# One FFT stream beside the first unit only, and Strassen's scheme for the second unit too

## The chip, the core and the metric

The kernel runs on one core of a Trainium2 chip. Times are device microseconds of one execution. TensorE (PE) does the matrix products, VectorE (DVE) and ScalarE (ACT) the element-wise work and the copies out of PSUM, GpSimd (POOL) some subtractions and additions between SBUF tiles. DMAs are issued on SP's queue (loads, outputs) and on ACT's (stores of results that are read again).

## The reference

Eight sequences of 3008 tokens and 256 channels go through a Fourier layer, and then through a mixer of tokens and channels.

```python
X = np.fft.rfft(x, axis=1)
Yr = X.real @ w_r - X.imag @ w_i + b_r
Yi = X.real @ w_i + X.imag @ w_r + b_i
Yr, Yi = (np.sign(Y) * np.maximum(np.abs(Y) - 0.01, 0) for Y in (Yr, Yi))
x = np.fft.irfft(Yr + 1j * Yi, n=3008, axis=1)          # (8, 3008, 256)

h = np.maximum(x.transpose(0, 2, 1) @ w_tok1, 0) @ w_tok2     # 3008 -> 256 -> 3008
u = x + h.transpose(0, 2, 1)
out = u + np.maximum(u @ w_ch1, 0) @ w_ch2                    # 256 -> 1536 -> 256
```

## The kernel before

**Precision.** A product is made from three matmuls in a 32-bit format of reduced precision: an operand is split into a high part (copied, by ACT as a rule) and the rest (a subtraction, by DVE or POOL), and `mm3` (lines 196 to 198) issues high x high, high x rest and rest x high.

**Units.** The eight sequences are five units: `[0]`, `[1]`, `[2, 3]`, `[4, 5]`, `[6, 7]`. A unit passes through a *spectral stream* (all that is done up to the token mixer's first product) and then through *channel mixing*.

**The spectral stream** of a unit is a generator, `spectral(u)`, that yields after each piece of PE work an estimate of its time. It first makes a DFT of length 47 in 13 groups (`dft47`: load `x`, sum and difference `sd`, split into `xh` and `xl`, PE product `p`, copy `a`, store to `a_d`). Units 3 and 4 have their DFT done within the steps of the unit before (`beside`). Then come 12 steps `kp`, with one or two sequences each: load `a`, PE `px` (`forward`), ACT copies `xf`, POOL adds a third part to `xf`, ACT and DVE split it into `xth` and `xtl`, PE `pm` (`mix`, the weights in the frequency domain), DVE `z` (bias and threshold), ACT and POOL split that into `y` and its rest (`yh`, `yl` with two sequences), PE `pi` (`inverse`) with the copy `bt` and its store to `b_d`, and PE `gp` (`tokens`). In unit 1 each step also splits the matrices `wt` (ACT, POOL) and `et` (ACT, DVE) and stores them for the later units. The stream ends with `g` in DRAM.

**Channel mixing** goes through a list of chunks of tokens. A token mix `make_u` (PE `pu`, line 860) makes the next chunk's `u` ahead of time from `wt2`, `g` and `b2`. There are two forms:

- `channel(n)`, chunks of up to 512 tokens: for each of 12 blocks of 128 features 6 matmuls of the first layer (`ph`), ACT and DVE make `hh` and `hlo` (lines 898, 899), and 6 matmuls of the second layer (`po`) two blocks later.
- `channel7(ns)`, chunks of up to 1024 tokens: Strassen's scheme for the first layer. For each pair of feature blocks, 7 products of 3 matmuls over half the tokens (`sx`, `sw`, `sq`, `sz`), with sums on DVE and copies on ACT between them (`sn`), in place of 8. The second layer is as before. `weigh` and `sum_u` make the summed operands.

Unit 0 is in 7 chunks of 470 or 376 tokens, since with it the float64 matrix `w_tok2` is read in pieces (`raw`), narrowed, split, and kept for the others. Unit 1 is in a chunk of 448 and five of 512. Units 2 to 4 are in wide chunks.

**Memory.** `raw`, `x` and `a` come from one ring of three buffers (`ld`). Before the first wide chunk the stream's pools are closed and their memory is taken by those of the Strassen stage (`open_seven`), so by then the stream has to be done. What is left of it at that point runs alone (`run(sp)`).

**What sets the order.** The loop at the end of the kernel draws on both generators. After each piece of mixing (an estimate `c`, counted down in `left_c`) it runs pieces of the stream while `left_s > pace * left_c`. `pace` is the ratio of what is left of the two, set anew after a `"wait"` (a unit's start), which holds the stream for 10 us of mixing. For unit 0 the stream's share is 2.1 times the estimate for a one-sequence unit; the rest lies beside unit 1.

Of the kernel before, what the change touches and what calls it, by code (L numbers as in the profile page):

```python
# [32 lines left out]
CW = 512  # L33
# [6 lines left out]
SPECTRAL = 70.3 + NG * (SLOW - 0.7)  # L40
# [86 lines left out]
def tile_kernel(ctx: ExitStack, tc: tile.TileContext, io):  # L127
# [650 lines left out]
    chunks = []  # L778
    for u, bs in enumerate(UNITS):
        total, at = N * len(bs), 0  # L780
        if u == 0:
            widths = [k * TOKS for k in sizes]
        elif u == 1:
            widths = [total % CW] + [CW] * (total // CW)
        else:
            plain = 0 if u == 2 else 0
            rest = total - plain
            widths = [plain % CW] * (plain > 0) + [CW] * (plain // CW) + [rest % CW7] + [CW7] * (rest // CW7)
        for cw in widths:
            chunks.append((u, at, cw))  # L790
            at += cw
        assert at == total
# [296 lines left out]
    def channel7(ns):  # L1089
        channels.close()  # L1090
        wc["tail"] = ctx.enter_context(tc.tile_pool(name="tail", bufs=1, reuse_waits="tile"))
        behind = None
        half = NF // 2
        for n in ns:
            after = n + 1 if n + 1 < len(chunks) else None
            mine = list(needs[after]) if after else []
            for p in range(half):
                hs = first7(n, p)
                if behind:
                    second7(*behind, 0, (0, 1))  # L1100
                if p < len(mine):
                    make_u(mine[p])
                    if p + 1 < len(mine):
                        load_wt2(mine[p + 1])
                        load_b2(mine[p + 1])
                if p == half - 2:
                    load_ahead(n + 2)
                if behind:
                    second7(*behind, 1, (0, 1))
                    if p == 0:  # L1110
                        for k in range(2):
                            finish7(behind[0], k, 2)
                behind = n, p, hs
                if after and p == half - 2:
                    sum_u(after)
                    for i in range(2):
                        split_u7(after, i)
                if after and p == half - 1:
                    for i in range(2, 7):
                        split_u7(after, i)  # L1120
        for k in range(2):
            for f in range(2):
                second7(*behind, f, (k,))
            finish7(behind[0], k, 2 - k)

    def run(gen):
        for _ in gen:
            pass
# [5 lines left out]
    spent, left_s, left_c, pace, hold = done, 0.0, 0.0, 0.0, None  # L1134
    first_wide = min(n for n, (_, _, cw) in enumerate(chunks) if cw > CW)

    def mixing(lo, hi):
        slots = sum(groups[g][3] for n in range(lo, hi) for g in needs[n + 1])
        return sum(32.7 * cw / CW for _, _, cw in chunks[lo:hi]) + 3.6 * slots * TOKS / GW

    for n, (u, at, cw) in enumerate(chunks):
        if n == first_wide:
            channel7(range(n, len(chunks)))
            break
        if at == 0 and u < 2:
            if u == 0:
                left_s = 2.1 * SPECTRAL - spent
                left_c = mixing(0, sum(cu == 0 for cu, _, _ in chunks))
            else:
                left_s = 3 * SPECTRAL + 4 * 70.3 - spent  # L1150
                left_c = mixing(n, first_wide - 1)
            pace, hold = 0.0, left_c - (25.0 if u == 0 else 0.0)
        for c in channel(n):
            if c == "end":
                if chunks[n + 1][2] > CW:
                    run(sp)
                    left_s = -1e9
                else:
                    while gts[u + 1] is None:
                        step = next(sp)  # L1160
                        if step != "wait":
                            left_s, spent = left_s - step, spent + step
                continue
            left_c -= c
            if hold is not None:
                if left_c > hold:
                    continue
                pace, hold = left_s / max(left_c, 1.0), None
            while left_s > pace * left_c:
                step = next(sp, None)  # L1170
                if step is None:
                    left_s = -1e9
                elif step == "wait":
                    hold = left_c - 10.0
                    break
                else:
                    left_s, spent = left_s - step, spent + step
# [36 lines left out]
```

## Time and profile before

| | |
|---|---|
| runs shown | 2396.96, 2398.89, 2388.59 us; median 2396.96 |
| the profiled execution | 2399.55 us, its span 2397.8 us |
| PE busy | 2360.6 us, 98% |
| DVE, ACT, POOL busy | 1417.6, 1143.3, 252.7 us |
| DMA | 277 MB, 116 GB/s in the mean |

The times agree within half a per cent, which is what one can hope to resolve. A matmul's row overlaps the next one, so a busy PE may still be one that is delayed a little at each step, and its cost is best read from the distance of the rows. The spectral stream can be told in any table by POOL, which does nothing else after the start.

### The profile page before, as it was taken

How to read it: one execution, taken by the hardware profiler on the slowest of the kernel's cores; microseconds unless marked ns; L12 is line 12 of the kernel's file. 1: busy time of each engine (PE TensorE's matmuls, PEld its weight loads, DVE VectorE, ACT ScalarE, POOL GpSimd, SP SyncE). 2: the span in 40 equal slices, each digit the busy share in tenths (PEclk: the TensorE clock that was granted, in tenths of full speed). 3: DMA queues.
4: the chain of work that ended last, by engine and by line, in shares of the span. 5: the costliest groups of instructions: out<-in, count | busy, mean ns of one | idle time of the engine just before them, and what ended most of it. 6: DMA issues, size and time to landing. Idle time of an engine off the chain costs nothing.

```text
span 2397.8 us, 32249 instructions
## 1 busy us (share of the span) xinstructions
PE 2360.6 (98%) x12524; PEld 2063.7 (86%) x12524; DVE 1417.6 (59%) x2220; ACT 1143.3 (48%) x2033; POOL 252.7 (11%) x223
## 2 busy tenths in 40 slices
PE   8999999999999999999999999999999999999999
PEld 7778899999988888898988888898888889888887
DVE  7966766655646564555555555555555555555554
ACT  6754445544434443433444444444444444444543
POOL 0000332232323322330000000000000000000000
PEclk9999999999999999999999999999999999999999
DMA  8765467655555545433213112122311112222100
GB/s 217 237 222 158 152 205 241 198 167 181 176 181 169 185 149 171 141 128 126 64 60 91 57 49 61 37 81 60 91 57 38 52 57 82 60 86 60 40 1 36
DMA packets 149766, 277.06 MB, mean 116 GB/s; under 512 B 10933, under 2 KB 94477, under 8 KB 149613
## 3 DMA queue, kind: packets, MB, share of 16 engines
q1 hardware_dynamic: 115225, 208.40, 29.5%
q10 hardware_dynamic: 34388, 66.60, 8.2%
q8 instruction: 99, 1.62, 0.3%
q14 instruction: 54, 0.44, 0.1%
HBM read 177.57 MB, written 97.39 MB: 115 GB/s over the span
## 4 chain that ended last, share of the span: by engine, by line
PE 87%; DVE 5%; DMA 3%; ACT 1%; issue 1%; POOL 1%; SPq 1%; ACTq 0%; DVEq 0%; POOLq 0%
PE po L196 10%; PE po L197 10%; PE po L198 10%; PE pu L860 5%; PE sx L196 3%; PE sx L197 3%; PE sx L198 3%; PE px L482 2%; PE ph L196 2%; PE ph L197 2%; PE ph L198 2%; PE sw L196 2%; PE pm L198 2%; PE sw L197 2%; PE sw L198 2%; PE pm L196 2%
## 5 line engine op out<-in xcount | busy, mean ns | idle before, releaser
L196 PE MATMUL po<-hh,w2h 128*128 128x512 f32 (+3 forms) x1176 | 453.4, 386 | 1.2 <-DVE o L965 0.9
L197 PE MATMUL po<-hlo,w2h 128*128 128x512 f32 (+3 forms) x1176 | 449.3, 382 | 1.1 <-DVE hlo L899 1.1
L198 PE MATMUL po<-hh,w2l 128*128 128x512 f32 (+3 forms) x1176 | 449.1, 382 | 0.0
L1032 ACT ACTIVATE hh<-sn 128x512 fp32r<-128x512 f32 (+1 forms) x432 | 270.7, 627 | 86.5 <-DVE sn L1052 56.8
L1033 DVE SCALAR_TENSOR_TENSOR hlo<-sn,hh 128x512 fp32r<-128x512 f32 (+1 forms) x432 | 291.0, 674 | 10.0 <-ACT hh L1032 0.6
L197 PEld LDWEIGHTS po<-hlo,w2h 128*128 128x128 f32 x1176 | 221.2, 188 | 38.3 <-DVE hlo L899 2.2
L196 PEld LDWEIGHTS po<-hh,w2h 128*128 128x128 f32 x1176 | 221.2, 188 | 38.1 <-ACT xf L484 1.0
L198 PEld LDWEIGHTS po<-hh,w2l 128*128 128x128 f32 x1176 | 221.0, 188 | 38.0
L1041 DVE TENSOR_TENSOR sn<-sq,sn 128x512 f32<-128x512 f32 (+1 forms) x108 | 73.4, 680 | 290.1 <-PE sq L198 266.8
L1037 ACT COPY sn<-sx 128x512 f32<-128x512 f32 (+1 forms) x108 | 62.5, 579 | 341.4 <-PE sx L198 341.3
L149 DVE TENSOR_TENSOR xtl<-xf,xth 128x768 fp32r<-128x768 f32 x84 | 85.1, 1013 | 117.9 <-ACT xth L146 117.8
L196 PE MATMUL pm<-wmh,xth 128*128 128x256 f32 x504 | 146.2, 291 | 4.8 <-ACT xth L146 3.0
L899 DVE SCALAR_TENSOR_TENSOR hlo<-ph,hh 128x512 fp32r<-128x512 f32 (+3 forms) x156 | 98.7, 636 | 82.6 <-ACT hh L898 82.1
L867 ACT COPY uf<-pu 128x470 f32<-128x470 f32 (+15 forms) x152 | 60.5, 425 | 178.3 <-PE pu L860 177.5
L198 PE MATMUL pm<-wmh,xtl 128*128 128x256 f32 x504 | 142.6, 285 | 0.8 <-DVE xtl L149 0.8
L197 PE MATMUL pm<-wml,xth 128*128 128x256 f32 x504 | 142.4, 283 | 0.0
L860 PEld LDWEIGHTS pu<-g,b 96*128 96x128 f32 x1024 | 133.1, 194 | 3.5
L898 ACT ACTIVATE hh<-ph 128x512 fp32r<-128x512 f32 (+3 forms) x156 | 86.4, 556 | 103.1 <-PE ph L198 91.9
L860 PE MATMUL pu<-g,b 96*128 96x94 f32 x1024 | 131.3, 274 | 0.0
L149 POOL TENSOR_TENSOR yl<-z,yh 128x512 fp32r<-128x512 f32 x72 | 95.9, 1332 | 274.2 <-ACT yh L146 268.1
L196 PE MATMUL ph<-uh,w 128*128 128x512 f32 (+3 forms) x312 | 118.9, 382 | 3.6 <-DVE hlo L899 2.7
L197 PE MATMUL ph<-ul,w 128*128 128x512 f32 (+3 forms) x312 | 116.2, 373 | 0.0
(185 smaller groups left out, 5223.6 us busy)
## 6 DMA issues: line engine op xcount, KB each, us to landing
wt<-wt_d SPq DMA_DIRECT2D x28, 940.0 KB, 5.8
x<-in_x SPq DMA_DIRECT2D x39, 480.0 KB, 4.9
wt<-ws_d SPq DMA_DIRECT2D x36, 512.0 KB, 4.3
a<-a_d SPq DMA_DIRECT2D x36, 512.0 KB, 5.5
b_d<-bt ACTq DMA_DIRECT2D x36, 512.0 KB, 5.5
a_d<-a ACTq DMA_DIRECT2D x36, 480.0 KB, 4.0
wt<-wt_d SPq DMA_DIRECT2D x21, 752.0 KB, 5.2
b<-b_d SPq DMA_DIRECT2D x32, 480.0 KB, 6.5
```

The source lines that it names most:

```text
L149: lo_eng.tensor_tensor(out=lo, in0=src, in1=hi.bitcast(F32), op=ALU.subtract)
L196: PE.matmul(out, lhsT=wh, rhs=xh, start=start, stop=False, skip_group_check=more)
L197: PE.matmul(out, lhsT=wh, rhs=xl, start=False, stop=False, skip_group_check=more)
L198: PE.matmul(out, lhsT=wl, rhs=xh, start=False, stop=stop, skip_group_check=more)
L860: PE.matmul(pt[:, s * TOKS:(s + 1) * TOKS], lhsT=b2[:, s, cs], rhs=g2[:, 0 if s0 + s == 0 else 1], start=False, stop=s == k - 1)
L867: S.copy(out=ufs[m][:, ct, lo - at:hi - at], in_=pt[:, lo - c0:hi - c0])
L898: S.activation(out=hh, in_=pt, func=AF.Relu)
L899: V.scalar_tensor_tensor(out=hlo, in0=pt, scalar=0.0, in1=hh.bitcast(F32), op0=ALU.max, op1=ALU.subtract)
L1032: S.activation(out=hh, in_=t, func=AF.Relu)
L1033: V.scalar_tensor_tensor(out=hlo, in0=t, scalar=0.0, in1=hh.bitcast(F32), op0=ALU.max, op1=ALU.subtract)
L1037: S.copy(out=snap[0], in_=x)
L1041: V.tensor_tensor(out=snap[0], in0=q, in1=snap[0], op=ALU.add)
```

## The change

Unit 1 gets wide chunks (960, 1024, 1024), so the first wide chunk is now its first and `channel` does unit 0 alone. The whole stream of units 1 to 4 gets one pace, over the six chunks of unit 0 that come before the switch of memory; the last chunk of unit 0 is the one in which the Strassen stage is prepared.

```diff
-        elif u == 1:
-            widths = [total % CW] + [CW] * (total // CW)
         else:
-            plain = 0 if u == 2 else 0
+            plain = 0 if u == 1 else 0
             rest = total - plain
             widths = [plain % CW] * (plain > 0) + ... + [rest % CW7] + [CW7] * (rest // CW7)
...
-        if at == 0 and u < 2:
-            if u == 0:
-                left_s = 2.1 * SPECTRAL - spent
-                left_c = mixing(0, sum(cu == 0 for cu, _, _ in chunks))
-            else:
-                left_s = 3 * SPECTRAL + 4 * 70.3 - spent
-                left_c = mixing(n, first_wide - 1)
-            pace, hold = 0.0, left_c - (25.0 if u == 0 else 0.0)
+        if n == 0:
+            left_s = 3 * SPECTRAL + 4 * 70.3 - spent
+            left_c = mixing(0, first_wide - 1)
+            pace, hold = 0.0, left_c - 25.0
```

What it moves shows in the order of instructions on each engine. On ACT, in the steps of unit 1's stream, `hh` is the mark of a block of mixing. Before:

```order
L898 ACTIVATE hh<-ph 128x470
L146 CAST y<-z 128x512
L536 COPY bt<-pi 128x512
L146 CAST et<-ef 128x256
L537 DMA b_d_93<-bt 32x8x256
L146 CAST wt<-aw 128x512
L376 DMA es_d<-et 128x512
L898 ACTIVATE hh<-ph 128x470
L376 DMA ws_d<-wt 128x1024
L484 COPY xf<-px 128x512
L146 CAST xth<-xf 128x768
```

The same place in the new order:

```order
L146 CAST wt<-aw 128x512
L376 DMA es_d<-et 128x512
L484 COPY xf<-px 128x512
L376 DMA ws_d<-wt 128x1024
L146 CAST xth<-xf 128x768
L536 COPY bt<-pi 128x512
L146 CAST et<-ef 128x256
L146 CAST y<-z 128x512
L537 DMA b_d_93<-bt 32x8x256
L146 CAST wt<-aw 128x512
L484 COPY xf<-px 128x512
```

Where a step had two blocks of mixing it now has one, or, as here, none.

On ACT again, in the steps of the last unit's stream. Before:

```order
L484 COPY xf<-px 128x512
L146 CAST xth<-xf 128x768
L484 COPY xf<-px 128x512
L146 CAST xth<-xf 128x768
L146 CAST yh<-z 128x2x256
L898 ACTIVATE hh<-ph 128x512
L146 CAST yh<-z 128x2x256
L536 COPY bt<-pi 128x512 x2
L537 DMA b_d_96<-bt 32x4x1024
L484 COPY xf<-px 128x512
L146 CAST xth<-xf 128x768
L898 ACTIVATE hh<-ph 128x512
```

And now:

```order
L146 CAST xth<-xf 128x768
L484 COPY xf<-px 128x512
L146 CAST xth<-xf 128x768
L146 CAST yh<-z 128x2x256
L536 COPY bt<-pi 128x512 x2
L537 DMA b_d_96<-bt 32x4x1024
L146 CAST yh<-z 128x2x256
L484 COPY xf<-px 128x512
L146 CAST xth<-xf 128x768
```

Of the last unit's 12 steps most have no block of mixing at all.

On DVE, behind the narrowing of a piece of `w_tok2` (`raw` to `wide`). Before, these stood beside unit 1's steps or the DFT of unit 2, here with mixing behind them:

```order
L169 TENSOR_TENSOR wide<-raw,wide 128x376
L170 TENSOR_TENSOR wide<-wide 128x376
L899 SCALAR_TENSOR_TENSOR hlo<-ph,hh 128x376
L149 TENSOR_TENSOR wt_4252<-wide,wt_4252 128x376 x2
L899 SCALAR_TENSOR_TENSOR hlo<-ph,hh 128x376 x4
L250 TENSOR_TENSOR sd<-x 120x512
```

In the new order three of the pieces stand within the steps of units 2 and 3:

```order
L169 TENSOR_TENSOR wide<-raw,wide 128x376
L168 TENSOR_SCALAR wide<-wide 128x376
L170 TENSOR_TENSOR wide<-wide 128x376
L169 TENSOR_TENSOR wide<-raw,wide 128x376
L149 TENSOR_TENSOR xtl<-xf,xth 128x768
L170 TENSOR_TENSOR wide<-wide 128x376
L149 TENSOR_TENSOR wt_4536<-wide,wt_4536 128x376 x2
L250 TENSOR_TENSOR sd<-x 120x512
L511 TENSOR_TENSOR z<-pm_4302,bias 128x512
```

There `sd<-x` waits for a load into the buffer that the first of these rows frees, and `z` of the running step stands behind it.

## The prediction

> **What bounds the kernel now.** I read the page first: span, busy times, the slices, and the chain that ended last.
>
> ```profile
> span 2397.8 us, 32249 instructions
> PE 2360.6 (98%) x12524; PEld 2063.7 (86%) x12524; DVE 1417.6 (59%) x2220; ACT 1143.3 (48%) x2033; POOL 252.7 (11%) x223
> POOL 0000332232323322330000000000000000000000
> PE 87%; DVE 5%; DMA 3%; ACT 1%; issue 1%; POOL 1%; SPq 1%; ACTq 0%; DVEq 0%; POOLq 0%
> ```
>
> TensorE is the bound, and 87% of the last chain is its own work. POOL works only for the spectral stream, so its digits show where that runs: slices 5 to 18, about 240 to 1085 us. Then the busy times by stage. The columns are the stretch, its length, the busy time and count of PE, PEld, DVE, ACT and POOL, the granted clock, the DMA share and GB/s.
>
> ```profile
> 180.00:380.00 200.00, 192.35 (x1192) 176.91 (x1191) 129.91 (x210) 89.35 (x162) 48.22 (x38) 1.00 0.58 182
> 380.00:480.00 100.00, 96.39 (x556) 90.21 (x555) 66.87 (x102) 53.20 (x93) 23.82 (x17) 1.00 0.72 208
> 480.00:900.00 420.00, 417.40 (x2488) 375.86 (x2487) 245.96 (x340) 196.97 (x323) 125.18 (x115) 1.00 0.57 173
> 900.00:960.00 60.00, 58.85 (x347) 51.88 (x346) 28.27 (x41) 22.91 (x41) 12.65 (x13) 1.00 0.53 168
> 960.00:1080.00 120.00, 120.00 (x760) 108.75 (x759) 70.63 (x102) 49.06 (x81) 37.34 (x34) 1.00 0.42 134
> 1080.00:1140.00 60.00, 60.00 (x295) 51.30 (x295) 35.99 (x56) 24.47 (x44) 2.71 (x2) 1.00 0.40 126
> 1140.00:2340.00 1200.00, 1200.00 (x5797) 1028.97 (x5797) 671.60 (x1040) 570.74 (x1047) 0.00 (x0) 1.00 0.20 60
> ```
>
> From 180 to 1080 us PE is idle for 7.65 + 3.61 + 2.60 + 1.15 = 15 us, nearly all of it in the stream of unit 1 (180 to 380) and at the first steps of a unit (380 to 480, 900 to 960). The Strassen stage from 1140 has no idle time, with DVE at 56%. So matmuls taken out there count in full. The waits of PE between 180 and 1080 (total, times, longest, in us) are short ones, on several feeders:
>
> ```profile
> PE pm L196 <- ACT xth L146: 3.0, 5, 1.1
> PE ph L196 <- DVE hlo L899: 2.7, 4, 1.2
> PE p L196 <- ACT xh L146: 1.6, 1, 1.6
> ```
>
> **What is removed.** The first layer of unit 1 (3008 tokens) takes 12 feature blocks x 2 x 3 = 72 matmuls for each chunk now. With Strassen's scheme a wide chunk has two halves and 6 pairs of feature blocks, and a pair takes 7 products x 3 = 21 matmuls of half the chunk's width. A matmul's cost is its distance to the next one, since its row (0.39 us) overlaps the next. Of each pair of rows the second is nine matmuls after the first.
>
> ```profile
> 1300.12 0.39 PE L197 MATMUL po<-hlo,w2h 128*128 128x512 f32 x1
> 1302.16 0.39 PE L197 MATMUL po<-hlo,w2h 128*128 128x512 f32 x1
> ...
> 1154.10 0.36 PE L198 MATMUL po<-hh,w2l 128*128 128x448 f32 x1
> 1155.92 0.37 PE L198 MATMUL po<-hh,w2l 128*128 128x448 f32 x1
> ```
>
> So 512 columns cost 2.04 / 9 = 0.2267 us, 448 cost 0.202, and 480 about 0.214 between them. Before: 72 x 0.202 + 360 x 0.2267 = 96.2 us. After, chunks of 960, 1024, 1024: 126 x 0.214 + 252 x 0.2267 = 84.1 us. That is 54 matmuls and **12.1 us less**. The second layer (3008 columns either way) and the 7 token mixes of unit 1 stay, within 0.3 us, so I take 11.7. The scheme's added sums and copies on DVE and ACT cost nothing: what hides them is the saturated PE of 1140 to 2340, where the same code runs with DVE 44% free.
>
> **What is moved.** The whole stream (some 480 us of PE's time: the 905 us from 180 to 1085 less some 425 for the mixing beside it, at the intervals above) now lies beside six of unit 0's seven chunks, not beside twelve. By counting matmuls in the new order, mixing falls from about 45% of PE's time there to 20 to 25%. It was the cover for the stream's latencies, so I go through the places where it gets thin.
>
> *DFT of unit 1* (10 groups left after the start). A group's result goes out through two buffers `a`: copy, issue, landing.
>
> ```profile
> L271 ACT COPY a<-p x38: 567/587/604, 195.8 to 467.8; 120x512 f32<-120x512 f32 x38
> a_d<-a ACTq DMA_DIRECT2D x12, 240.0 KB, 2.9
> ACT a L271 <- DMA a_d<-a: 6.5, 3, 2.5
> 194.00:222.00 28.00, 26.07 (x146) 23.16 (x146) 21.51 (x44) 16.61 (x32) 0.00 (x0) 1.00 0.65 180
> ```
>
> The loop is 0.59 + 0.3 + 2.9 = 3.8 us for two groups, so 19 us for ten. Before, 28 us of PE time hid it, with 1.9 idle. In the new order the ten have about 13 us of PE work (60 matmuls of 256 columns and some 26 of mixing), and the first two buffers are free. Ends: -1.9 (the idle time goes) to +6. I take **+3**, near the loop's end since ACT already waited for that landing.
>
> *Steps of unit 1's stream.* Each has PE work of 36 matmuls of 256 columns (0.12 us each by the slope above) and `px` (0.8, an estimate), 5.1 us. POOL and ACT pass the step in order:
>
> ```profile
> L149 POOL TENSOR_TENSOR y<-z,y 128x512 fp32r<-128x512 f32 x5 | 6.6, 1324 | 22.7 <-ACT y L146 22.7
> L149 POOL TENSOR_TENSOR wt<-aw,wt 128x512 fp32r<-128x512 f32 x4 | 5.3, 1322 | 4.7 <-ACT wt L146 4.7
> L485 POOL TENSOR_TENSOR xf<-xf 128x256 f32<-128x256 f32 x5 | 4.3, 862 | 11.0 <-ACT xf L484 11.0
> L146 ACT CAST xth<-xf 128x768 fp32r<-128x768 f32 x5 | 4.2, 836 | 5.0 <-POOL xf L485 5.0
> L146 ACT CAST y<-z 128x512 fp32r<-128x512 f32 x5 | 3.1, 621 | 6.6 <-DVE z L519 6.6
> L536 ACT COPY bt<-pi 128x512 f32<-128x512 f32 x5 | 2.9, 581 | 0.0
> L146 ACT CAST et<-ef 128x256 fp32r<-128x256 f32 x5 | 2.1, 412 | 0.0
> 283.00:336.00 53.00, 53.00 (x356) 50.05 (x355) 29.27 (x45) 23.85 (x44) 15.28 (x14) 1.00 0.53 178
> ```
>
> In the new order `xf`, `xth`, `bt`, `et`, `y` on ACT, `y` and `wt` on POOL, and the next `xf` follow one another: 0.86 + 0.84 + 0.58 + 0.41 + 0.62 + 1.32 + 1.32 = 6.0 us. Before, a step took 53 / 5 = 10.6 us of PE time with the mixing, and PE never idled in the stretch. After, steps of 5.1 and 7.7 alternate (12.8 against 12.0, covered), and about four stand with no mixing at all: 4 x 0.9. Ends: -2 to 12 x 0.9 = +11. I take **+3**, from the counted bare steps.
>
> *DFT of unit 2.* Its 13 groups move 480 KB in and 480 KB out each, in about 57 us of PE work by the new order (4.4 us a group, where 382 to 444 gave 5.2). That is 219 GB/s, and some 270 with the chunk's own loads and stores.
>
> ```profile
> 382.00:444.00 62.00, 59.69 (x319) 54.86 (x318) 45.62 (x70) 37.24 (x66) 15.87 (x9) 1.00 0.72 207
> 460.00:480.00 20.00, 18.70 (x133) 17.81 (x132) 15.71 (x24) 10.45 (x17) 6.21 (x7) 1.00 0.80 238
> ```
>
> At 238 GB/s the transfers would need 65 us (+8); if DMA goes on to a share of 0.9, only the idle 2.3 us of 382 to 444 is at stake (-2.3). I take **+2**, near the lower end: a share of 0.8 still leaves room.
>
> *Units 2 and 3.* Three of unit 0's `wt2` pieces are now loaded and narrowed beside the two-batch streams. Their two `raw` tiles take two of the three buffers that `x` and `a` use, and SP's queue stands behind them. The next `x` can be issued only after the last reader of `raw` on DVE, which then has eight other instructions before it wants that `x`: an estimate of 4.4 us, at about 0.5 each beside `xtl` (0.96).
>
> ```profile
> x<-in_x SPq DMA_DIRECT2D x39, 480.0 KB, 4.9
> L149 DVE TENSOR_TENSOR xtl<-xf,xth x84: 943/959/1278, 241.4 to 1076.1; 128x768 fp32r<-128x768 f32 x84
> ```
>
> With the landing of 4.9 us and the issue, `x` is about 1 us late each time: **+3** (0 to +9, if each stops PE for 3 us).
>
> *Unit 4.* By its rule of paces the stream leaves the last unit nearly bare: about 115 us with six feature blocks in it. A stretch like that stands in the trace:
>
> ```profile
> 1041.20:1057.10 15.90, 15.90 (x112) 14.55 (x111) 11.23 (x16) 8.08 (x13) 5.53 (x5) 1.00 0.43 150
> L485 POOL TENSOR_TENSOR xf<-xf x84: 726/739/1413, 239.1 to 1074.5; 128x256 f32<-128x256 f32 x84
> L149 POOL TENSOR_TENSOR yl<-z,yh x72: 1264/1292/1872, 470.5 to 1083.9; 128x512 fp32r<-128x512 f32 x72
> ```
>
> That is 15.9 us without a feature block, and no idle time on PE. Ends: 0, as there, to 11 steps x 0.7 = +8, if the POOL instruction ahead of each `xth` is at its longest (1413 for 739 ns) and PE waits for it. I take **+2**, for the unit's first steps, since 900 to 960 idled 1.15 us at the same place.
>
> *Passage into the Strassen stage.* DVE's 36 us of 1080 to 1140 now meet a chunk of 376 tokens with three token mixes, 39 us: **+1** (0 to +4). Less mixing beside the stream also means fewer changes between the two: **-1**.
>
> POOL's `xf` has a median of 739 ns and a longest of 1413. The Trainium skill (SBUF — State Buffer, "Who interferes with whom") says that a VectorE instruction with two SBUF inputs and a GpSimd instruction that reads SBUF exclude each other for a whole instruction; the trace agrees by that 1413. By the Trainium skill's rule in full, with 1.41 for 0.86 in each of unit 1's steps, the loop there is 6.55 us, the four bare steps cost 6 us in place of 3, and the sum is 3 us higher.
>
> **The sum.** The profiled execution took 2399.55 us (span 2397.8, 1.75 around it). 2399.55 - 11.7 + 3 + 3 + 2 + 3 + 2 + 1 - 1 = 2400.9. The median of the runs shown is 2.6 below that execution, so I forecast **2398 us**: no change. Within 0.5% (12 us) a measurement can hardly tell it from none.
>
> **The rivals.**
>
> *The feeders keep up* (chance 0.20). The six terms are nothing and some of the 15 us of idle time goes with the stretch that holds it: -11.7 to -16, so 2381 to 2385. For it: 960 to 1080 and 1041 to 1057, dense and never idle. Against: 180 to 480, where half the mixing did not hide all.
>
> *POOL sets the pace of unit 1's steps* (0.17), the slower side. Beside a DVE with less idle time `xf`, `y` and `wt` go to the longest seen above, 1.41 and 1.87 us. The loop is then 6.0 + 3 x 0.55 = 7.65 us: 2.5 too long for each of four pairs of steps and 2.55 for each of four bare ones, 20 us in place of 3, so 2398 + 17 = 2415. It makes the kernel slower by over 12 us when `y` on POOL has a mean above some 1.7 us. Against it: the means of 283 to 336 stand near the medians. The Trainium skill's rule above would be its cause.
>
> *A starved DFT halves the clock* (0.05). It happened once where PE had gaps:
>
> ```profile
> 150.00:160.00 10.00, 7.61 (x33) 6.72 (x32) 5.54 (x12) 3.97 (x8) 0.00 (x0) 0.71 0.87 258
> 160.00:170.00 10.00, 10.00 (x41) 8.88 (x41) 5.32 (x11) 7.04 (x14) 0.00 (x0) 0.78 0.27 82
> ```
>
> If two such spells follow the DFTs, at some 5 us each with the starvation of +6 and +8 at their ends, the time is about 2417. The Trainium skill (TensorE: Matmul & The Clock Gate, "Part 1: The HAM clock gate") has the clock follow how busy PE was lately; the lower clock after the idle 2.4 us here agrees.
>
> That the stream isn't within the mixing at all is partly so already (the bare last unit), and is in the terms.
>
> **How the numbers follow.** Forecast within 12 us: 0.58. Feeders keep up: 0.20, nearly all of it over 0.5% faster. POOL 0.17 and clock 0.05: slower by over 0.5%. So faster 0.18, same 0.61, slower 0.21. The range of 2384 to 2414 goes from most of the first rival to just below the second one's centre.
>
> **What would show it.** Right: 54 matmuls fewer, POOL's digits ending near slice 15, Strassen rows from about 925 us, PE idle for 25 to 30 us in the stream. Each term by its place: waits of PE's `p` on `xh` in the DFTs, of `pm` on `xth` in unit 1, PE at 100% in the bare unit 4, DVE waiting for `x` after each `raw`. Wrong: idle time above 40 us, POOL's `y` over 1.7 us in the mean, a granted clock under 0.95 after 240 us, or idle time back at 15 us or less, which makes it faster.

## The result: 1.5% slower, and the profile after

The changed kernel takes **2430.3 us** (median; 2427.4 to 2434.6), the kernel before 2396.1 beside it: a ratio of 1.0149 (1.0120 to 1.0178). The forecast was 2398, no change, and its range ended at 2414. The two profiled executions lie closer together, 28.9 us. Page of the changed kernel: span, busy times, POOL's slices, the chain.

```profile
span 2426.7 us, 32485 instructions
PE 2365.3 (97%) x12470; PEld 2052.0 (85%) x12470; DVE 1481.3 (61%) x2313; ACT 1192.3 (49%) x2120; POOL 267.5 (11%) x223
POOL 0001543333342430000000000000000000000000
PE 82%; DVE 5%; DMA 4%; ACT 3%; POOL 3%; issue 3%; SPq 1%; ACTq 0%; DVEq 0%; POOLq 0%
```

The 54 matmuls are gone (12470 for 12524) and POOL's digits end in slice 15, both as forecast. But PE's own share of the chain fell from 87% to 82%. Busy times by stage say where; columns are the stretch, its length, PE, PEld, DVE, ACT, POOL, clock, DMA share, GB/s. First the kernel before (DFT of unit 2, then units 2 and 3), then the changed one: part of the DFT of unit 1, DFT of unit 2, units 2, 3 and 4, the bare steps of unit 4, the start of the Strassen stage, and the stream as a whole.

```profile
382.00:460.00 78.00, 75.69 (x417) 70.82 (x416) 49.55 (x76) 42.40 (x76) 17.60 (x10) 1.00 0.70 201
460.00:703.00 243.00, 241.70 (x1460) 221.34 (x1459) 136.27 (x194) 110.75 (x184) 66.72 (x61) 1.00 0.59 181
703.00:926.00 223.00, 220.40 (x1286) 194.47 (x1285) 132.26 (x180) 104.66 (x172) 65.22 (x60) 1.00 0.59 180
```

```profile
200.00:210.00 10.00, 6.09 (x28) 5.04 (x28) 6.55 (x14) 4.94 (x9) 0.00 (x0) 0.79 0.75 237
324.00:387.00 63.00, 52.47 (x208) 39.77 (x207) 39.42 (x43) 31.68 (x51) 23.35 (x12) 0.89 0.76 230
387.00:587.00 200.00, 190.68 (x1155) 169.40 (x1154) 139.21 (x197) 101.95 (x168) 70.72 (x60) 1.00 0.64 196
587.00:779.00 192.00, 185.97 (x1178) 170.89 (x1177) 126.29 (x185) 100.14 (x164) 73.17 (x61) 1.00 0.67 206
779.00:954.00 175.00, 171.38 (x1116) 158.24 (x1116) 114.65 (x168) 77.82 (x131) 54.18 (x48) 1.00 0.48 153
810.00:900.00 90.00, 90.00 (x604) 83.17 (x604) 60.05 (x85) 41.95 (x68) 37.91 (x34) 1.00 0.49 161
960.00:1020.00 60.00, 60.00 (x298) 52.59 (x298) 34.49 (x57) 30.27 (x59) 0.00 (x0) 1.00 0.14 39
180.00:960.00 780.00, 740.94 (x4552) 666.86 (x4552) 517.33 (x746) 382.54 (x641) 264.76 (x217) 0.99 0.62 193
```

PE is idle for 39 us from 180 to 960, where 15 us of idle time stood before in the stream. The DFT of unit 2 went from 2.3 to 10.5 us of idle time and to a clock of 0.89; unit 2 from 1.3 to 9.3; unit 3 from 2.6 to 6.0.

Idle time misses what a slow clock and a matmul held up in the pipeline cost. So I also work out a **delay**: for each matmul row its distance to the next, less the usual distance of that form (the 40th percentile of all its rows in the run), summed over a stage. It is taken from one execution of each kernel. Another way to group the rows moves every sum down by some 12 us and the differences between versions by about 1, so only the differences count. In us, with the mixing beside the stream (usual distances of `ph`, `po`, `pu`, from the first group of unit 1's DFT to the Strassen stage):

| run | time | mixing | DFT 1 | unit 1 | DFT 2 | unit 2 | unit 3 | unit 4 | sum |
|---|---|---|---|---|---|---|---|---|---|
| before | 2396.1 | 457 | 14.6 | 7.8 | 4.8 | 6.1 | 7.6 | 6.1 | 47.0 |
| **changed** | 2430.3 | 239 | 16.9 | 9.6 | 20.4 | 16.9 | 12.5 | 11.2 | 87.4 |
| e1 stream alone | 2439.6 | 239* | 16.6 | 9.4 | 20.9 | 17.2 | 13.3 | 10.8 | 88.2 |
| e2 three `ev` | 2426.3 | 239 | 18.0 | 9.4 | 19.6 | 18.5 | 13.4 | 11.0 | 89.8 |
| e3 four `ld` | 2427.7 | 239 | 12.5 | 10.2 | 20.1 | 19.8 | 10.4 | 11.0 | 84.0 |
| e4 more in the DFTs | 2434.2 | 239 | 10.2 | 8.9 | 8.7 | 22.9 | 31.4 | 12.4 | 94.4 |
| e5 raw within a block | 2452.2 | 239 | 19.1 | 10.1 | 27.4 | 14.9 | 27.8 | 11.2 | 110.7 |
| e6 no raw pieces | 2412.3 | 239 | 16.6 | 9.4 | 11.6 | 12.9 | 10.4 | 11.2 | 72.2 |
| e7 `sd` on DVE | 2428.0 | 239 | 16.6 | 9.0 | 16.2 | 17.8 | 13.9 | 11.3 | 84.7 |
| e8 e4 + e5 + e7 | 2420.5 | 239 | 8.0 | 8.8 | 10.1 | 15.4 | 25.6 | 12.4 | 80.2 |
| e9 bare units 2 to 4 | 2426.1 | 239 | 9.3 | 7.2 | 3.5 | 22.9 | 26.1 | 14.0 | 82.9 |
| e10 filler | 2433.8 | 239 | 18.3 | 9.3 | 11.3 | 17.6 | 12.6 | 11.2 | 80.3 |
| e11 1128 tokens | 2420.8 | 372 | 15.2 | 11.7 | 13.1 | 17.7 | 8.1 | 4.9 | 70.7 |
| e12 2068 tokens | 2424.2 | 304 | 17.2 | 11.8 | 9.6 | 20.2 | 11.0 | 5.7 | 75.6 |
| e13 before, one pace | 2393.8 | 456 | 12.0 | 3.9 | 5.5 | 11.3 | 7.3 | 5.1 | 45.0 |
| e14 e11, mixing early | 2407.3 | 371 | 11.6 | 15.3 | 4.2 | 11.8 | 9.9 | 6.0 | 58.9 |
| e15 mixing early | 2435.7 | 239 | 8.8 | 5.1 | 1.4 | 41.9 | 18.6 | 14.6 | 90.3 |

(* without unit 1's plain chunks, which follow the stream there.)

The delay grew by 40.4 us up to the Strassen stage and by 1.5 in it, and fell by 1.0 ahead of the stream; with the 11.7 us of saved matmuls that is +29.2, against 28.9 between the two spans. The 1.5 is the least certain: by other groupings it is near 0.

In the DFT of unit 2 the waits (engine, line, cause: total, times, longest) and POOL's rows show a feeder chain with no slack:

```profile
POOL sd L249 <- DVE xl L149: 30.2, 8, 16.1
ACT a L271 <- DMA a_d<-a: 14.9, 7, 5.7
PEld p L197 <- DVE xl L149: 8.1, 10, 1.7
```

```profile
327.40 5.97 POOL L249 TENSOR_TENSOR sd<-x 120x512 f32<-120x512 f32 x2 [16.14 <-DVE xl L149]
...
353.22 1.79 POOL L249 TENSOR_TENSOR sd<-x 120x512 f32<-120x512 f32 x1 [2.23 <-DVE xl L149]
356.17 1.79 POOL L249 TENSOR_TENSOR sd<-x 120x512 f32<-120x512 f32 x1 [1.16 <-DVE xl L149]
359.13 1.76 POOL L249 TENSOR_TENSOR sd<-x 120x512 f32<-120x512 f32 x1 [1.17 <-DVE xl L149]
```

A group takes 2.96 us where nothing else delays it (356.17 to 359.13): POOL's `sd`, then DVE's `xl`, one after the other. Two things make that chain. `sd` has two buffers, so POOL waits for an earlier group's `xl`. And where `xl` meets POOL's `sd` (353.22 to 355.01), it takes 2.26 us in place of 1.23:

```profile
353.83 2.26 DVE L149 TENSOR_TENSOR xl<-sd,xh 120x1024 fp32r<-120x1024 f32 x1
```

The first two `sd` took 2.98 each, while DVE narrowed a raw piece. ACT waited 14.9 us for stores of `a`.

In unit 2, SP's queue shows what the raw pieces do to `x`:

```profile
408.30 0.34 SPq L452 DMA_DIRECT2D x<-in_x  x1
412.37 0.35 SPq L179 DMA_DIRECT2D raw<-in_wt  x1
421.09 0.33 SPq L179 DMA_DIRECT2D raw<-in_wt  x1
442.40 0.35 SPq L452 DMA_DIRECT2D x<-in_x  x1
```

No `x` is issued for 34 us. The two tiles stay in the ring until their last readers, at 460.3 and 461.5, and `a` and `x` share the third buffer. Three feature blocks, the distance from load to narrowing, take that long when mixing is thin.

### The profile page after: what moved, and what is told of

Read it like the earlier page. It is cut to its first block, busy times and chain, and to the rows that moved or that the text cites. A ratio compares the mean times of both kernels' runs of the same rounds, so it can differ in the third digit from the quotient of the medians.

```text
span 2426.7 us, 32485 instructions
## 1 busy us (share of the span) xinstructions
PE 2365.3 (97%) x12470; PEld 2052.0 (85%) x12470; DVE 1481.3 (61%) x2313; ACT 1192.3 (49%) x2120; POOL 267.5 (11%) x223
## 4 chain that ended last, share of the span: by engine, by line
PE 82%; DVE 5%; DMA 4%; ACT 3%; POOL 3%; issue 3%; SPq 1%; ACTq 0%; DVEq 0%; POOLq 0%
PE po L196 10%; PE po L197 10%; PE po L198 10%; PE pu L858 4%; PE sx L196 4%; PE sx L197 3%; PE sx L198 3%; PE sw L196 2%; PE sw L198 2%; PE sw L197 2%; PE px L482 2%; PE pu L196 2%; PE pu L197 2%; PE pu L198 2%; PE pm L198 2%
## 5 line engine op out<-in xcount | busy, mean ns | idle before, releaser
L196 PE MATMUL po<-hh,w2h 128*128 128x512 f32 (+4 forms) x1176 | 454.0, 386 | 1.0 <-ACT hh L896 1.0
L197 PE MATMUL po<-hlo,w2h 128*128 128x512 f32 (+4 forms) x1176 | 449.6, 382 | 2.3 <-DVE hlo L897 2.3
L198 PE MATMUL po<-hh,w2l 128*128 128x512 f32 (+4 forms) x1176 | 449.1, 382 | 0.0
L1030 ACT ACTIVATE hh<-sn 128x512 fp32r<-128x512 f32 (+2 forms) x504 | 315.9, 627 | 99.4 <-DVE sn L1050 66.0
L1031 DVE SCALAR_TENSOR_TENSOR hlo<-sn,hh 128x512 fp32r<-128x512 f32 (+2 forms) x504 | 339.2, 673 | 10.9
L1039 DVE TENSOR_TENSOR sn<-sq,sn 128x512 f32<-128x512 f32 (+2 forms) x126 | 85.6, 679 | 333.7 <-PE sq L198 299.3
L1035 ACT COPY sn<-sx 128x512 f32<-128x512 f32 (+2 forms) x126 | 72.9, 579 | 398.9 <-PE sx L198 398.8
L865 ACT COPY uf<-pu 128x470 f32<-128x470 f32 (+11 forms) x146 | 60.1, 436 | 168.7 <-PE pu L858 167.9
L1044 DVE TENSOR_TENSOR sn<-sw,sn 128x512 f32<-128x512 f32 (+2 forms) x126 | 85.6, 679 | 70.7 <-PE sw L198 62.5
L146 ACT CAST xth<-xf 128x768 fp32r<-128x768 f32 x84 | 70.1, 834 | 99.2 <-POOL xf L485 99.1
L1041 ACT COPY sn<-sx 128x512 f32<-128x512 f32 (+2 forms) x126 | 73.1, 580 | 81.1 <-PE sx L198 81.1
```

What stands on the lines that cost most here:

```text
L146: S.copy(out=hi, in_=src)
L196: PE.matmul(out, lhsT=wh, rhs=xh, start=start, stop=False, skip_group_check=more)
L197: PE.matmul(out, lhsT=wh, rhs=xl, start=False, stop=False, skip_group_check=more)
L198: PE.matmul(out, lhsT=wl, rhs=xh, start=False, stop=stop, skip_group_check=more)
L1030: S.activation(out=hh, in_=t, func=AF.Relu)
L1031: V.scalar_tensor_tensor(out=hlo, in0=t, scalar=0.0, in1=hh.bitcast(F32), op0=ALU.max, op1=ALU.subtract)
```

## The experiments

All are edits of the changed kernel unless said otherwise; the diffs show the main lines. My first theory (T1): the loss is idle PE in the two DFTs, where the mixing got thin. Rivals: POOL's order in unit 1's steps; raw tiles in the ring of three; a cost of the wide chunks themselves.

**e1: the stream's half of the change alone.**

```diff
+        elif u == 1:
+            widths = [total % CW] + [CW] * (total // CW)
...
-            left_c = mixing(0, first_wide - 1)
+            left_c = mixing(0, 6)
```

> Only half of the change: the whole stream runs beside unit 0's first six chunks, as after the change, but unit 1 keeps its plain chunks (448 and five of 512), without Strassen's scheme. If the loss comes from the stream having too little mixing beside it (my theory), the idle time up to about 960 us stays and only the 11.7 us of saved matmuls go: 2430 + 12 = 2442 us, idle time of PE from 180 to 960 about 39 us as before. If the loss came from unit 1's wide chunks themselves (the passage into the Strassen stage, DVE there), the time falls back to about 2396 to 2400.

2439.6 us, 1.0192 (1.0176 to 1.0207), and the delays of the changed kernel stage by stage. The loss is in the stream. Strassen's scheme for unit 1 saves about what was forecast: 1.0192 less 1.0149 is 10 us, for 11.7, give or take 8 by the intervals. The rows are closer: at the usual distances those of e1 sum to 2295.0 us, as before the change, those of the changed kernel to 2283.3.

**e2 and e3: one more buffer for results, or for loads.**

```diff
-        return wk.tile(shape, F32, tag="ev", name=name, bufs=2)
+        return wk.tile(shape, F32, tag="ev", name=name, bufs=3)
...
```

```diff
-            raw = wk.tile([rows, n, 2], U32, tag="ld", name="raw", bufs=3)
+            raw = wk.tile([rows, n, 2], U32, tag="ld", name="raw", bufs=4)
...
-        return wk.tile(shape, F32, tag="ld", name=name, bufs=3)
+        return wk.tile(shape, F32, tag="ld", name=name, bufs=4)
...
```

> The change with three instead of two buffers for the results a and bt that ACT copies out and that are stored to DRAM (memory for it: tiles of the channel mixing cut from 512 to unit 0's 470 columns, four instead of five early raw tiles). Theory A, the two buffers pace the DFTs of units 1 and 2 (copy, issue, landing: ACT waits 15 us for the landing of a in the DFT of unit 2): those two stages lose 10 + 20 us now and would lose about 12 together, and the clock stays up: 2430 - 18 = 2412 us. Rival B, the DMA engines bound the DFT of unit 2 (share 0.97 in two of its 10 us slices): the stage stays as long, since the same bytes move: 2425 to 2430. Rival C, x loads and the subtraction on POOL bound it: 2428 to 2432.

> The change with four instead of three buffers in the ring that x, a and the raw tiles of unit 0's weights share (memory from the same cuts as for the third result buffer). If the raw tiles that lie in that ring hold up the next x (no x is issued from 408 to 442 us, where the pieces are read), the steps of unit 2 between 374 and 510 us lose about 6 in place of 15.6, and unit 3's start 2 less: 2430 - 11 = 2419 us. If the ring is not what delays these steps: 2428 to 2432.

2426.3 (1.0131, 1.0114 to 1.0149) and 2427.7 (1.0144, 1.0127 to 1.0161): too little for either theory. (To make room, both also cut tiles of the mixing from 512 to 470 columns and have four early raw tiles for five.) In e3 the hold-up of `x` was not gone: with four buffers none was issued from 395.5 to 426.0, so e3 says little about what it costs. In e2 ACT's wait in the DFT of unit 2 did go, and the next feeder stood behind it (waits, then POOL's rows):

```profile
ACT a L271 <- DMA a_d<-a: 3.0, 1, 3.0
PEld p L197 <- DVE xl L149: 13.7, 11, 4.4
...
343.03 1.80 POOL L249 TENSOR_TENSOR sd<-x 120x512 f32<-120x512 f32 x1 [1.16 <-DVE xl L149]
345.99 1.80 POOL L249 TENSOR_TENSOR sd<-x 120x512 f32<-120x512 f32 x1 [1.16 <-DVE xl L149]
348.95 1.80 POOL L249 TENSOR_TENSOR sd<-x 120x512 f32<-120x512 f32 x1 [1.16 <-DVE xl L149]
```

The stage was as long as before, 63 us, and the time lies in the range of rival B. From 335 to 365 the DMA engines of e2 were busy for 0.97, 0.98 and 0.90 of each 10 us, and DVE for 9.90 of the 10 from 345. So in the stage's middle the DMA engines and the pair of POOL and DVE both stand near their limit, and no run here tells which of them sets the pace.

**e4: more mixing beside the DFTs.**

```diff
-SLOW = 1.75
+SLOW = 5.25
```

> The change with one number altered: the estimate for a DFT group that paces the two generators, SLOW, 5.25 in place of 1.75. By the order, the mixing beside the DFT of unit 2 rises from 25 to 41 us of PE work and that beside the DFT of unit 1 by 8 us; it is taken from units 2 to 4. Theory: the two DFTs lose 30 us now because the loops of loads, copies and stores take longer than the PE work there; with 23 us more work in them they lose about 10, no spell of half clock follows in the DFT of unit 2, and the steps of units 2 to 4 lose some 3 more: 2430 - 17 = 2413 us. If what costs the time is thin mixing anywhere alike, what is won there is lost in units 2 to 4: 2425 to 2435.

The DFTs' delay fell by 18.4 us, near the 20 forecast, and 2434.2 us came out (1.0165, 1.0150 to 1.0180): units 2 and 3 lost 25 more. T1 alone falls: the loss in the DFTs can be moved, not removed. The worst place in unit 3 is a raw piece's time. POOL:

```profile
710.83 4.53 POOL L149 TENSOR_TENSOR yl<-z,yh 128x512 fp32r<-128x512 f32 x1 [6.36 <-ACT yh L146]
```

and DVE beside it, six of its rows of narrowing:

```profile
711.05 0.55 DVE L167 SCALAR_TENSOR_TENSOR wide<-wide 128x376 uint32<-128x376 uint32 x1
...
712.04 0.55 DVE L167 SCALAR_TENSOR_TENSOR wide<-wide 128x376 uint32<-128x376 uint32 x1
712.50 0.55 DVE L169 TENSOR_TENSOR wide<-raw,wide 128x376 f32<-128x376 f32 x1
712.96 0.35 DVE L168 TENSOR_SCALAR wide<-wide 128x376 uint32<-128x376 uint32 x1
713.23 0.55 DVE L170 TENSOR_TENSOR wide<-wide 128x376 f32<-128x376 f32 x1
713.69 0.55 DVE L169 TENSOR_TENSOR wide<-raw,wide 128x376 f32<-128x376 f32 x1
```

`yl` takes 4.53 us, 1.29 in the median before the change, while DVE works without a gap, and `pi` waits for it.

**e5 to e8: the raw pieces and the subtraction.** e5 loads and narrows a piece within one block, e6 leaves the late ones out (it loads the first piece's narrowed weights in their place, so its results are not the reference's), e7 takes POOL out of unit 2's DFT, e8 is e4, e5 and e7 together.

```diff
# e5
-                    if mine:
+                    if mine and seven:
                         load_wt2(mine[0])
+                if f == 4 and mine and not seven:
+                    load_wt2(mine[0])
...
-                    if i == 0 and f == 3:
+                    if i == 0 and f == (3 if seven else 5):
```

```diff
# e6
+        if u == 0 and g >= 3:
+            w = wk.tile([128, 4, 480], F32R, name="wt2", bufs=1)
+            DMA.dma_start(out=w[:, :, :k * TOKS].bitcast(F32), in_=wt2_d[:, :, :k * TOKS])
+            wts[g] = w
-        if u == 0:
+        elif u == 0:
```

```diff
# e7
...
-            yield from dft47(p.load_unit, p.a, p.w, 3, V if u == 1 else G)
+            yield from dft47(p.load_unit, p.a, p.w, 3, V)
```

> The change with the pieces of unit 0's weights loaded at feature block 4 and narrowed at block 5 of a chunk, in place of 0 and 3. Theory R: with thin mixing three blocks take long (raw tiles hold two of the ring's three buffers from 412 to 460, 546 to 586 and 725 to 759 us, 30 to 48 us each, 20 before the change), so the x and a of units 2 and 3 come one by one; one block takes a third of that, and the loss in units 2 and 3 (29 us now, 14 before the change) falls to about 18: 2430 - 11 = 2419 us. Rival: the narrowing itself, on ACT and DVE, costs the time, wherever it stands: 2427 to 2432.

> The change without reading and narrowing the last four pieces of unit 0's weights: in their place 940 or 752 KB of already narrowed weights (those of the first piece) are loaded, so the results are not the reference's. It gives the whole price of these pieces: raw buffers, narrowing and splitting on ACT and DVE. Theory R or its rival, either: units 2 and 3 lose 14 in place of 29 and the DFT of unit 2 starts without DVE's burst (3 less): 2430 - 18 = 2412 us. If the thin mixing costs the time for other reasons (waits within the steps themselves): 2425 to 2430.

> The change with both halves of sd of unit 2's DFT on DVE, none on POOL. In the DFT of unit 2 with three result buffers the groups followed each other by 2.96 us: POOL's sd of 1.80 (1.29 when alone) and DVE's xl of 1.16, one after the other, and xl took 1.8 to 2.3 where the two met. Theory S, the two engines exclude each other there: without POOL a group needs 0.69 + 0.69 + 1.2 = 2.6 us on DVE and the first two groups no longer 2.98 each, so the stage's loss falls from 20 to about 14: 2424 us. Rival, the stores of a and the loads of x bound the stage (DMA share 0.97): 2428 to 2431.

> Three edits on the change together: SLOW 5.25 (more mixing beside the DFTs), the pieces of weights loaded and narrowed within one block, and sd of unit 2 on DVE alone. With SLOW alone the DFTs lost 19 in place of 37 us, but units 2 and 3 lost 54 in place of 29, and there the waits stand in the time of the raw tiles. If theory R holds, the latter falls to about 20: 2430 - 18 - 9 = 2403 us. If the raw tiles are not the cause: 2430 to 2434.

e6's time came out as forecast, **2412.3 us** (1.0078, 1.0063 to 1.0094): the four late raw pieces cost 18 us, half the loss against the kernel before. (The kernel before was not run without them, so how much of this it pays too is not known.) The parts came out otherwise: units 2 and 3 were to lose 15 us less and lost 6.1 less, the DFT of unit 2 was to lose 3 less and lost 8.8 less. That the sum agrees is luck. The DFT of unit 2 and unit 2, then unit 2's first 40 us, its steady steps and the turn to unit 3:

```profile
323.00:377.00 54.00, 48.05 (x207) 36.89 (x206) 34.27 (x34) 29.86 (x49) 18.72 (x11) 0.97 0.79 237
377.00:572.00 195.00, 189.25 (x1149) 170.47 (x1148) 126.64 (x170) 97.25 (x157) 68.82 (x61) 0.99 0.68 208
377.00:417.00 40.00, 36.34 (x229) 32.18 (x228) 31.07 (x41) 21.61 (x34) 18.86 (x15) 0.96 0.69 201
417.00:557.00 140.00, 140.00 (x856) 126.61 (x855) 88.75 (x120) 71.33 (x116) 48.23 (x45) 1.00 0.66 200
557.00:602.00 45.00, 40.03 (x251) 36.02 (x250) 27.34 (x38) 20.65 (x34) 14.51 (x13) 1.00 0.62 183
```

So without raw pieces the steady thin steps lose nothing, and what units 2 and 3 still lose stands where a unit begins: some 7 us of delay in each of the two places, 2 to 3 in the same places before the change.

e5 failed, 2452.2 (1.0239, 1.0224 to 1.0254). One block is no short time where the stream has precedence: from the load to the last reader of its first tile it took 32 us (330 to 362, within the DFT of unit 2; 21 us of delay until 8 us after) and 76 us (555 to 631, at the start of unit 3, 16 us). The piece from 469 to 485, amid steady steps, had 0.5 at most. By these three, it is the place of a raw piece that counts; none of them isolates it. e7, 2428.0 (1.0140, 1.0115 to 1.0164): 4 us less in the DFT of unit 2, the rest as it was, within what can be told; inconclusive on the time. e8, 2420.5 (1.0112, 1.0092 to 1.0132), is the fastest version of the whole change that computes the whole result, 17 above its forecast: unit 3 still lost 25.6.

**e9: all mixing early, units 2 to 4 bare.**

```diff
+        k = 1.14 if u == 1 else 0.047
...
-                yield 0.9
+                yield k * 0.9
...
-            left_s = 3 * SPECTRAL + 4 * 70.3 - spent
+            left_s = 3 * NG * SLOW + 1.14 * 61.2 + 0.047 * 403.6 - spent
```

> The change, with the mixing of unit 0 given to the first part of the stream alone: weights on the stream's estimates (1.14 for unit 1's steps, 0.047 for the steps of units 2 to 4, SLOW as it was). By the order, 68 us of mixing lie beside the DFT of unit 1, 84 beside unit 1's steps and 49 beside the DFT of unit 2, about as before the change (68, 76, 56); all four late pieces of unit 0's weights are read there, and the steps of units 2 to 4 are bare. Theory: thin cover costs time in the DFTs and where raw tiles lie in the ring, and bare steps cost little (0.9 to 1.5 us of delay in 30 us, as in unit 4). Then the DFT of unit 2 loses 6 (20 now), the DFT of unit 1 14, unit 1's steps 8, units 2 and 3 18 (29 now): 2430 - 14 - 3 - 2 - 11 = 2400 us or less, and the bare stretch shows PE at 98%. Rival: bare steps of units 2 and 3 lose more than thin ones, since the DFT of the next unit lies in them (POOL's sd and DVE's xl beside yl and xtl): 2420 to 2440.

2426.1 us (1.0130, 1.0113 to 1.0146), 26 above the theory; the rival holds. DFT of unit 2, then units 2 and 3:

```profile
383.00:453.00 70.00, 68.70 (x380) 64.43 (x379) 46.20 (x67) 38.80 (x68) 16.12 (x10) 1.00 0.76 227
453.00:617.00 164.00, 151.63 (x942) 134.33 (x940) 110.21 (x153) 90.37 (x140) 70.46 (x61) 0.98 0.68 208
617.00:781.00 164.00, 146.11 (x919) 130.38 (x919) 110.26 (x148) 88.75 (x137) 71.62 (x61) 0.96 0.69 217
```

The DFT is healed (1.3 us idle) and the bare units, which carry the next unit's DFT as well, idle for 12.4 and 17.9 us, with no raw piece in them (the last is read out at 435). Unit 4's bare steps, with PE at 90.00 of 90, were no model for them.

**e10: filler matmuls in the DFT of unit 2.**

```diff
+                    for _ in range(fill):
+                        PE.matmul(pt[:, o:o + w], lhsT=f1r[:, 0, i], rhs=wmh[:120, 0].rearrange("p t c -> p (t c)"), start=True, stop=True)
...
```

> The change with 52 filler matmuls of 512 columns in the DFT of unit 2 (four for each group, on weights that are at hand, in the bank that the group's own product overwrites): 52 x 0.2267 = 11.8 us of added PE work, results the same. If the stage is paced by its feeders, the filler lies in PE's idle time (20 us there) and costs at most 2; if the two spells of half clock there (6.8 us each) are an own cost, they go with the gaps, and 3 to 5 us come back: 2426 us. If the stage were bound by PE: 2430 + 12 = 2442.

2433.8 us (1.0164, 1.0147 to 1.0181).

```profile
325.00:391.00 66.00, 58.89 (x262) 48.81 (x262) 37.11 (x42) 32.16 (x50) 23.41 (x12) 0.95 0.71 218
```

Of 11.8 us of filler the stage shows 3 (66 us for 63); some 9 lie in idle time. (The 3.5 between the two times is within their intervals.) The clock rose from 0.89 to 0.95 and nothing came back. But one of the stage's two spells of half clock stayed, and the DFT of unit 1 was slower by the clock (0.66 from 195 to 215, 0.83 in the changed kernel). So I found no cost of the half clock beside that of the gaps, and cannot say that it has none.

**e11 and e12: part of unit 1.** Widths `[344, 512, 512, 512, 564, 564]` and `[428, 512, 692, 688, 688]` for unit 1, one pace.

> A part of the change: 1128 tokens of unit 1 go through Strassen's scheme (two chunks of 564), 1880 stay plain (344 and three of 512), and the stream runs at one pace beside all ten chunks before the last plain one. By the order PE's work falls by 4.8 us against the kernel before (11.4 in the whole change). Mixing beside the stream is about 335 us, against some 405 before and 190 after the change. Theory L, the loss goes in proportion to the cover taken away (41 us for 215): 13 us here, so 2395 - 5 + 13 = 2403 us. Theory K, the loss starts only where the cover is so thin that DFTs and raw tiles starve: about 3 us here, so 2393 us.

> A larger part: 2068 tokens of unit 1 through Strassen's scheme (692, 688, 688), 940 plain (428, 512). PE's work falls by 8.4 us, mixing beside the stream is about 260 us. Theory L: a loss of 28 us, 2395 - 8 + 28 = 2415 us. Theory K: 15 us or less, 2402 us.

2420.8 (1.0107, 1.0092 to 1.0122) and 2424.2 (1.0119, 1.0102 to 1.0136). Neither theory: the first 85 us of mixing taken away cost most. That left open whether the one pace, and not the amount, does it.

**e13 to e15: place or amount.** e13 is the kernel before with the one pace, e14 is e11 and e15 the whole change with mixing early (weights as in e9).

```diff
# e13, on the kernel before
-        if at == 0 and u < 2:
...
+        if n == 0:
+            left_s = 3 * SPECTRAL + 4 * 70.3 - spent
+            left_c = mixing(0, first_wide - 1)
+            pace, hold = 0.0, left_c - 25.0
# e14
+        k = 0.8 if u == 1 else 0.4
# e15, with e7's edit
+        k = 0.5 if u == 1 else 0.095
```

> The kernel before with only the other half of the change: unit 1 plain as before, but one pace for the whole stream over all chunks ahead of the switch of memory, in place of two phases (which lay 2.1/6.8 of the stream's estimate beside unit 0, so thickly). By the order, mixing beside the DFT of unit 1 falls from 68 to 58 us, beside unit 1's steps from 76 to 54, beside the DFT of unit 2 from 56 to 44; units 2 to 4 get 45 us more. If it is the amount of mixing beside the stream that counts (405 us here as before): within 3 us of 2395. If its place counts, since the DFTs and the raw tiles are where it is needed: some 12 to 20 us slower, 2407 to 2415, with the loss in the DFT of unit 2 and the first steps of unit 2.

> The part of the change with 1128 tokens of unit 1 in Strassen's scheme (2420.8 us with one pace), with weights on the stream's estimates (0.8 for unit 1's steps, 0.4 for those of units 2 to 4) that put the mixing early: 68, 64 and 57 us beside the two DFTs and unit 1's steps, as before the change, the rest thinner. Theory of place: the loss of the DFTs and of unit 2 falls from 46 to about 27, 2420.8 - 20 = 2401 us, and no raw tile is left for unit 2. Theory of amount: unchanged, 2416 to 2424.

> The whole change with weights (0.5 for unit 1's steps, 0.095 for those of units 2 to 4): 71, 48 and 60 us beside the DFT of unit 1, unit 1's steps and the DFT of unit 2, about 26 left for units 2 to 4; and sd of unit 2 on DVE alone. The DFTs and unit 1's steps then lose 22 in place of 47 us, units 2 to 4 more than the 34 of the change, up to the 63 of the version with bare steps: 2430 - 25 + 15 = 2420 us. If it comes below 2410, thin steps with no raw tile are cheap after all.

e13: 2393.8 us, 0.9996 (0.9984 to 1.0007). With all of unit 1 as cover, the pace makes no difference.

e13 and e1 together are the plainest test of the cover. Both have unit 1's plain chunks and one pace, and both do the same work (busy times of e1, then of e13):

```profile
PE 2378.8 (98%) x12524; PEld 2064.9 (85%) x12524; DVE 1428.8 (59%) x2220; ACT 1142.7 (47%) x2033; POOL 268.0 (11%) x223
PE 2359.7 (99%) x12524; PEld 2061.8 (86%) x12524; DVE 1420.8 (59%) x2220; ACT 1144.9 (48%) x2033; POOL 251.3 (10%) x223
```

All that differs is over how much mixing the pace spreads the stream: `mixing(0, 6)` against `mixing(0, first_wide - 1)`. The spans, 2437.4 and 2394.3, are 43.1 us apart, and the delays 43.2.

e14: 2407.3 (1.0052, 1.0038 to 1.0067), 13 better than e11, so with less cover the place does count, though by less than the 20 of its theory. e15: 2435.7 (1.0174, 1.0158 to 1.0190), 16 above its forecast. DFT of unit 2 and unit 2, of e13 and then of e15:

```profile
342.00:409.00 67.00, 64.77 (x309) 56.50 (x308) 48.47 (x71) 39.06 (x67) 17.15 (x10) 0.97 0.72 221
409.00:666.00 257.00, 253.62 (x1558) 236.83 (x1556) 150.59 (x216) 116.02 (x198) 69.86 (x62) 0.99 0.58 178
```

```profile
347.00:425.00 78.00, 78.00 (x412) 71.93 (x411) 52.59 (x83) 41.99 (x74) 0.00 (x0) 1.00 0.69 211
425.00:627.00 202.00, 176.72 (x1057) 156.03 (x1056) 126.20 (x175) 95.52 (x153) 73.51 (x62) 0.96 0.62 190
```

e15's DFT has no idle time at all, and the unit after it 25.3 us. Of the whole change, eight versions that only place the mixing or the feeders otherwise (e2 to e5, e7 to e9, e15) have delays of 80 to 111 us. No version tried beats the kernel before; e13 equals it.

**What is settled.** The loss is the price of the cover (e1 against e13): 457 us of mixing beside the stream hold the delay at 45 to 47 us, some 370 at 59 to 71, 304 at 76, 239 at 80 or more as long as the raw pieces are read. The late raw pieces are 18 us of the time of the changed kernel. **What stays open** is the split of the rest (a delay of 72 in e6 against 47) among `a`, `x`, POOL, DVE and the DMA engines, since each took the other's place, what holds PE up where a unit begins, and why unit 1's steps lost 12 to 15 us in e11 and e14 but 3.9 in e13.

## Why the prediction was wrong

- *PE's saved work, -11.7:* right (e1, 10 us).
- *DFT of unit 1, +3:* right, +2.3.
- *Unit 1's steps, +3:* right, +1.8. The rival that had POOL set the pace is wrong, since `y` stayed under 1.7 us (240 to 330 us):

```profile
L149 POOL TENSOR_TENSOR y<-z,y 128x512 fp32r<-128x512 f32 x11 | 14.9, 1357 | 24.0 <-ACT y L146 24.0
```

- *DFT of unit 2, +2:* **failed, +15.6.** The step that failed is the PE work set against the feeders: it was counted as 57 us, and the trace has 43 (25 of mixing, 18 of `p`). The feeders' time was near: 65 us at the upper end, where the stage took 63. That is luck in part, since it came from 238 GB/s as the bound, and the stage reached 334. The term then took the lower end. What the runs show in its place: with PE's 43 us the stage (first `p` to unit 2's first `px`) took 63 with three buffers `a` too (e2), so the wait of 14.9 us in that loop did not set it; 59 with `sd` on DVE (e7); 66 with 11.8 us more work for PE (e10); and 54 without the raw piece, whose narrowing falls on the stage's start (e6). That piece, which the term left out, is 8.8 of the 15.6.
- *Units 2 and 3, +3:* **failed, +15.7** (10.8 and 4.9), beyond the upper end of +9. The mechanism, raw tiles in the ring and a late `x`, was named, but it is the smaller part: without the raw pieces (e6) the units lose 23.3 us, with them 29.4, before the change 13.7. So the pieces are 6.1 of the 15.7. I took one late `x` for each piece, 1 us; the tiles stay for three feature blocks, and thin mixing made these 48 us long (412 to 460), yet DVE waited only 2.1 us for that `x`. The pieces' DVE work also holds POOL. The other 9.6 had no term: they stand in the first steps of unit 2 and at the turn to unit 3, a loss that I had priced for unit 4 alone.
- *Unit 4, +2:* mis-sized, +5.1 (within its end of +8), in its first steps and at its end; the bare stretch itself ran at 100%, as forecast.
- *Passage, +1:* right as far as can be told, 0 to +1.5. The -1 for fewer changes between the two shows in no row.
- *The starved DFT with half the clock (0.05):* it happened, three times (0.79 at 200 to 210; 0.66 in two stretches below), and the sign named for it, a clock under 0.95 after 240 us, came. The time is above its 2417, but by the delays of all stages, and e10 found no price of the clock beside that of the gaps.

```profile
330.00:340.00 10.00, 7.12 (x18) 4.86 (x19) 5.73 (x6) 5.07 (x8) 5.16 (x3) 0.66 0.66 182
360.00:370.00 10.00, 6.61 (x17) 5.28 (x18) 4.78 (x4) 5.17 (x9) 2.67 (x2) 0.66 0.67 202
```

Behind the terms stands one error: each stage was priced at full speed of one feeder, with the others as they ran under thick cover. The densest stretch of the trace, unit 4, has neither a DFT beside it nor raw pieces, and was taken as evidence for stages that have both. The terms together were +13 and came to some +40.

## What to carry to other kernels

Work that hides latencies has a price, and it can be read as delay per us of cover taken away: here 0.14 to 0.28 us for the first 85 (11.9 and 23.7 us of delay, e14 and e11), against 12 us saved for all 218 (0.055). Before taking it away, list for each stage beside it all in-order feeders and every buffer that is held *for a count of the hiding work's steps*, since these holds lengthen as that work thins. If moving the cover from one stage to the next only moves the loss, look for more cover or for a feeder less (as e6 tried), not for a better pace.

## What had not been expected of the hardware

POOL and DVE stood in each other's way far beyond the 1.41 us that the prediction took from the trace of before: `sd` 2.98 and, in e4, `yl` 4.53 us (1.30 and 1.29 in the median before the change) beside DVE's narrowing. In the changed kernel `sd` has a median of 1.73 us. The trace of before had single cases of this size too, which the prediction missed: its longest `sd` took 3.27 us and its longest `y` 3.06. The Trainium skill (SBUF — State Buffer, "Who interferes with whom") has the two share a port pair that the first taker holds for its whole instruction. The `xl` of 2.26 us, begun while POOL's `sd` ran and ended 1.08 us after it, agrees. Why `yl` was held over a whole run of short DVE instructions is not shown here. The prediction priced this rule in unit 1's steps alone; it bit in the DFT of unit 2 and where raw pieces are narrowed.

DMA reached 334 GB/s at a share of 0.97 in the DFT of unit 2 (the prediction took 238 as the bound, and the most it quoted was 258 at 0.87):

```profile
340.00:350.00 10.00, 8.48 (x34) 5.66 (x34) 7.46 (x8) 5.63 (x10) 6.18 (x4) 1.00 0.97 334
```
